# Two attentions on one core: V in products of 512 columns, PSUM banks shared, V moved to the start of a unit

## The chip, the core and the metric

The kernel runs on one core of a Trainium2 chip. The core has a matrix engine (TensorE, "PE" in the profile, with its weight loader "PEld" and its sequencer "PEq"), VectorE (DVE), ScalarE (ACT), GpSimd (POOL) and a queue engine (SyncE, SP). Transfers are issued from ScalarE's queue (ACTq) and SyncE's queue (SPq). Products go into PSUM, which has eight banks of 512 fp32 columns per partition; ScalarE and VectorE read them from there. The metric is the device time of one execution in microseconds (us), as the median over runs.

## The reference: two attentions, side by side

Two independent inputs x (2048 x 1024) each go through a projection to q, k and v, an attention with 32 heads of 32 columns, and an output projection; the two results are concatenated. They differ in which keys a query sees:

```python
# A: 8 keys, at distances 0, 2, 4 ... 14 behind the query
off = jnp.arange(W) * dil                      # W, dil = 8, 2
logits = jnp.einsum("bhsd,bhswd->bhsw", q, kg) * scale
logits = jnp.where(mask[None, None, :, :], logits, -1e9)
o = jnp.einsum("bhsw,bhswd->bhsd", _softmax(logits), vg)

# B: the 256 keys up to and including the query
mask = (idx[:, None] - idx[None, :] >= 0) & (idx[:, None] - idx[None, :] < W)   # W = 256
scores = jnp.where(mask[None, None], scores, -1e9)
o = jnp.einsum("bhqk,bhkd->bhqd", _softmax(scores), v)
# both: o.transpose(...).reshape(B, S, D) @ wo
```

## The kernel before

**Units and groups.** The work is cut into 8 units of 512 rows: four of B ("dense"), then four of A, whose rows are sorted into even and odd so that its 8 keys become neighbours ("window"). A unit has 8 groups (NG) of 4 heads. `attention` (L560) makes the steps of a group; `window` replaces its second half for A.

**Split products.** Each fp32 operand is split into a rounded high part and a low remainder (`parts`, L117: a cast on L120, a subtraction on L125 on GpSimd or L128 on VectorE). Each product is done three times (TERMS: high-high, high-low, low-high). Projections split weights and x; for the scores the three terms are stacked on 96 partitions by transfers on SyncE's queue (L308), so that one product does all of them.

**The steps.** `qk_items` (L343) computes q and k of a group: for each of them 8 slices of the contraction (NK), each of 3 products of 512 columns, into one bank. `evac` (L294, L298) takes them out and issues the stacking; parts of k that the next chunk needs go through `halo` buffers in DRAM (L288, L313). `v_items` (L387) computes V for two groups at a time, a "part": 8 slices, two banks, in each bank two row blocks of 256 columns, 3 products each. Here x is the stationary operand and the weights move. There are four parts to a unit; `vbuf` keeps six row blocks of each, since a dense chunk looks 256 rows back. `o_items` (L426) is the output projection of the unit before, 8 blocks of 8 slices.

**The attention of a group.** `first` (L585) makes 16 score tiles; each lies in a bank until VectorE has masked it and taken the row maximum (L590) and ScalarE has taken exp and its sum (L595). `log_sum` and `rows` (L608 to L631) bring the logarithms of the sums into two extra rows of the stacked q. `second` (L667, window L480) makes the scores again, transposed and already normalised; ScalarE takes exp (L672, L485), masks follow on VectorE or GpSimd (L653, L656, L495), and `values` (L712, L519) multiplies with V. `finish` (L548, L552) writes the split output `ot`.

**The order.** Nothing is scheduled at run time: while the kernel is built, a `Clock` keeps estimated times of all engines, and a loop at the end takes, out of four sequences (aux, second scores and values, first scores, projections), the item that is ready first; on a tie the projections come last. So projections fill the gaps between scores. The order of the projections is the list `plan`, made from `V_SLOTS = {0: 0, 1: 1, 5: 2, 7: 3}` (V part 0 after q and k of group 0, and so on) and `O_SLOTS`. `Stream` loads weights and x in that order through three raw buffers on ScalarE's queue (L94) and splits them a little ahead. `x_items` brings the next unit's x in the middle of the last V part.

**PSUM.** Seven banks are two rings: `rg`, three banks for projections, and `rs`, four banks for scores (`NS = 4`); the eighth, `ro`, takes the values.

Of the kernel before, what the change touches and what calls it, by code (L numbers as in the profile page):

```python
# [14 lines left out]
P = 128  # L15
# [64 lines left out]
class Stream:  # L80
# [10 lines left out]
    def load_to(self, n):  # L91
        while self.loaded < min(n, len(self.items)):
            raw = self.raws.tile([P, 1024], F32, tag="raw", name="raw")
            self.nc.scalar.dma_start(raw, self.items[self.loaded][1])  # L94
            self.raw[self.loaded] = raw, self.ck.load(1.9, self.ck.now)
            self.loaded += 1
# [20 lines left out]
    def parts(self, t, raw, t0):  # L117
        nc, ck = self.nc, self.ck
        n = raw.shape[1]
        nc.vector.tensor_copy(t[:, 0, :], raw)  # L120
        end = r = ck.use("dve", n / 1920 + 0.16, t0)
# [16 lines left out]
def kernel(ctx, tc, xs, wqk, wv, wo, outs, units):  # L138
# [14 lines left out]
    psg = ctx.enter_context(tc.tile_pool(name="psg", bufs=7 - NS, space=PSUM))  # L153
    pss = ctx.enter_context(tc.tile_pool(name="pss", bufs=NS, space=PSUM))
# [23 lines left out]
    def unit_x(u):  # L178
        for g in range(4):
# [6 lines left out]
    for p in plan:  # L186
# [3 lines left out]
        elif p[0] == "v":  # L190
            for g in range(2):
                item(p + (g,), "w", wv[ly, 2 * p[2] + g])
# [4 lines left out]
        else:  # L197
            item(("qk", p[1], 0, 0), "w", wqk[units[p[1]][0], 0])
            unit_x(p[1])
# [39 lines left out]
    vbuf = [const.tile([P, 6, 256], F32, name=f"vbuf{i}") for i in range(4)]  # L239
# [6 lines left out]


# [18 lines left out]
    rg, rs, ro = Ring(psg, 7 - NS, "g"), Ring(pss, NS, "s"), Ring(pso, 1, "o")  # L266
# [11 lines left out]
    def qk_items(u, s):  # L278
# [45 lines left out]
        for t in range(2):  # L324
# [13 lines left out]
            def run(k, t=t, h=h):  # L338
# [3 lines left out]
                for i, (a, b) in enumerate(TERMS):  # L342
                    nc.tensor.matmul(h["ps"], h["w"][:, a, k * P:(k + 1) * P], xt[u][k][:, b, :],  # L343
                                     start=(k == 0 and i == 0), stop=(k == NK - 1 and i == 2))
                if k == 3 and st.items[min(where["qk", u, s, t] + 1, len(st.items) - 1)][0] != "x":
# [21 lines left out]
    def v_items(u, part):  # L367
# [3 lines left out]
        h = {}  # L371

        def ready(k, b):
            if k % 4 == 0 and b == 0:
                st.split_to(where["v", u, part, k // 4] + 1)
                h["r"] = st.ready[where["v", u, part, k // 4]]
            return latest(h["r"], rg.when()) if k == 0 else h["r"]

        def run(k, b):
            if k == 0:  # L380
                h[b] = rg.take()
            if k % 4 == 0 and b == 0:
                h["w"] = st.get(where["v", u, part, k // 4])[0].rearrange("p a (k f) -> p a k f", k=4)
# [457 lines left out]
```

## Time and profile before

| | |
|---|---|
| median of 3 runs | 1996.71 us |
| the three runs | 1998.98, 1987.27, 1996.71 us |
| profiled execution, its own time | 1983.01 us |
| its span | 1980.9 us |
| mean granted TensorE clock | 0.987 |
| VectorE, ScalarE, GpSimd busy | 65%, 48%, 30% of the span |
| TensorE products | 12608 records |

Durations in the profile are of one execution. "Busy" is the time covered by an engine's instructions; a matrix product's bar is longer than the distance to the next one's start, since products are pipelined. A group's row gives the line and engine, output and input by the program's names, shapes, count, busy time, mean of one in ns, and the idle time before it with what ended it. In the timeline the columns are start, duration, engine, line, operation and count, with idle time before it in brackets. A window gives busy time and count of each engine, then the granted clock, the share of the transfer engines and GB/s.

### The profile page before, as it was taken

How to read it: one execution, taken by the hardware profiler on the slowest of the kernel's cores; microseconds unless marked ns; L12 is line 12 of the kernel's file. 1: busy time of each engine (PE TensorE's matmuls, PEld its weight loads, DVE VectorE, ACT ScalarE, POOL GpSimd, SP SyncE). 2: the span in 40 equal slices, each digit the busy share in tenths (PEclk: the TensorE clock that was granted, in tenths of full speed). 3: DMA queues.
4: the chain of work that ended last, by engine and by line, in shares of the span. 5: the costliest groups of instructions: out<-in, count | busy, mean ns of one | idle time of the engine just before them, and what ended most of it. 6: DMA issues, size and time to landing. Idle time of an engine off the chain costs nothing.

```text
span 1980.9 us, 36437 instructions
## 1 busy us (share of the span) xinstructions
PE 1925.2 (97%) x12608; PEld 1620.0 (82%) x12608; DVE 1284.9 (65%) x3700; ACT 952.4 (48%) x3125; POOL 593.0 (30%) x717
## 2 busy tenths in 40 slices
PE   8999999999999999999999999999999999999998
PEld 6877887888877888788888888978898888878886
DVE  5667775678775777566865667645686557655562
ACT  3466464566554656555563344423444334423441
POOL 3333333334333343433342221222222221222121
PEclk9999999999999999999999999999999999999998
DMA  5545546455446465344635546445563656444442
GB/s 175 155 125 141 178 123 177 133 162 168 120 142 186 123 184 137 119 147 146 170 114 150 165 151 188 130 132 172 145 190 114 181 165 180 138 146 134 141 137 75
DMA packets 136503, 294.93 MB, mean 149 GB/s; under 512 B 14464, under 2 KB 42112, under 8 KB 136320
## 3 DMA queue, kind: packets, MB, share of 16 engines
q1 hardware_dynamic: 85632, 124.82, 25.5%
q10 hardware_dynamic: 50688, 167.79, 24.5%
q8 instruction: 100, 1.64, 0.3%
q14 instruction: 83, 0.68, 0.1%
HBM read 163.58 MB, written 27.26 MB: 96 GB/s over the span
## 4 chain that ended last, share of the span: by engine, by line
PE 81%; DVE 9%; DMA 6%; ACT 2%; issue 2%; SPq 0%; ACTq 0%; DVEq 0%
PE g L343 31%; PE g L426 16%; PE g L387 14%; PE s L585 7%; PE s L667 4%; PE o L712 3%; PE s L480 3%; PE o L519 2%; DMA qst<-rt 2%; DVE x L128 1%; DVE w L120 1%; DVE w L128 1%; DMA kst<-nat 1%; ACT s L595 1%; DVE s L590 1%
## 5 line engine op out<-in xcount | busy, mean ns | idle before, releaser
L343 PE MATMUL g<-x,w 128*128 128x512 f32 x3072 | 797.7, 400 | 8.5 <-DVE w L120 8.1
L125 POOL TENSOR_TENSOR w<-raw,w 128x512 fp32r<-128x512 f32 x231 | 404.1, 1749 | 1127.1 <-DVE w L120 778.9
L343 PEld LDWEIGHTS g<-x,w 128*128 128x128 f32 x3072 | 561.2, 191 | 112.6 <-DVE w L120 8.4
L595 ACT ACTIVATE s<-s,nm 128x384 f32<-128x384 f32 (+3 forms) x1024 | 451.8, 442 | 287.0 <-DVE nm L590 271.6
L387 PE MATMUL g<-w,x 128*128 128x256 f32 x3072 | 412.7, 285 | 0.0
L426 PE MATMUL g<-ot,w 128*128 128x512 f32 x1536 | 391.5, 399 | 3.6 <-DVE w L120 2.9
L387 PEld LDWEIGHTS g<-w,x 128*128 128x128 f32 x3072 | 391.6, 191 | 2.0 <-issue 1.0
L426 PEld LDWEIGHTS g<-ot,w 128*128 128x128 f32 x1536 | 285.6, 191 | 57.5 <-DVE w L120 3.6
L590 DVE CUSTOM_DVE_ANT_0 s<-s,mask_d 128x384 f32<-128x384 f32 (+2 forms) x512 | 261.4, 556 | 77.2 <-PE s L585 76.1
L585 PE MATMUL s<-kst,qst 96*128 96x384 f32 (+3 forms) x1024 | 236.3, 304 | 22.4 <-issue 7.9
L653 POOL TENSOR_SCALAR_AFFINE_SELECT pbuf<-pbuf 128x128 f32<-128x128 f32 (+1 forms) x451 | 179.4, 419 | 193.7 <-ACT pbuf L672 188.7
L672 ACT ACTIVATE pbuf<-s 128x384 f32<-128x384 f32 (+2 forms) x480 | 198.8, 504 | 78.0 <-PE s L667 66.3
L585 PEld LDWEIGHTS s<-kst,qst 96*128 96x128 f32 x1024 | 180.3, 193 | 64.5 <-issue 21.7
L590 DVE CUSTOM_DVE_ANT_0 s<-s,mask_w 128x136 f32<-128x136 f32 (+1 forms) x512 | 142.4, 323 | 117.1 <-PE s L585 115.8
L595 ACT ACTIVATION_READ_ACCUMULATOR s<-s,nm 128x1 f32 x1024 | 209.8, 205 | 0.0
L120 DVE CAST w<-raw 128x1024 fp32r<-128x1024 f32 x256 | 197.5, 771 | 10.4 <-PE g L426 10.4
L128 DVE TENSOR_TENSOR w<-raw,w 128x512 fp32r<-128x512 f32 x281 | 195.0, 701 | 8.8
L294 ACT ACTIVATE nat<-g 128x512 fp32r<-128x512 f32 x128 | 76.6, 598 | 248.7 <-PE g L343 212.2
L298 DVE SCALAR_TENSOR_TENSOR nat<-g,nat 128x512 fp32r<-128x512 f32 x128 | 88.3, 690 | 152.2 <-ACT nat L294 136.8
L495 DVE TENSOR_TENSOR pbuf<-pbuf,keep_w 128x272 f32<-128x272 f32 (+1 forms) x224 | 116.2, 564 | 52.5 <-ACT pbuf L485 51.7
L590 DVE DVE_READ_ACCUMULATOR2_ANT nm<- 128x1 f32 x1024 | 145.1, 142 | 0.0
L667 PEld LDWEIGHTS s<-qst,kst 98*128 98x128 f32 x704 | 107.5, 189 | 40.7 <-ACT s L595 15.8
(44 smaller groups left out, 1050.7 us busy)
## 6 DMA issues: line engine op xcount, KB each, us to landing
raw<-wqk ACTq DMA_DIRECT2D x128, 512.0 KB
qst<-nat SPq DMA_DIRECT2D x192, 256.0 KB
kst<-nat SPq DMA_DIRECT2D x192, 256.0 KB
raw<-wv ACTq DMA_DIRECT2D x64, 512.0 KB
raw<-wo ACTq DMA_DIRECT2D x64, 512.0 KB
raw<-xs ACTq DMA_DIRECT2D x32, 512.0 KB
outs<-ost ACTq DMA_DIRECT2D x64, 256.0 KB
halo<-nat SPq DMA_DIRECT2D x40, 256.0 KB
```

The lines of the kernel that those rows point to most:

```text
L120: nc.vector.tensor_copy(t[:, 0, :], raw)
L125: nc.gpsimd.tensor_tensor(o, a, b, op=ALU.subtract)
L128: nc.vector.tensor_tensor(o, a, b, op=ALU.subtract)
L343: nc.tensor.matmul(h["ps"], h["w"][:, a, k * P:(k + 1) * P], xt[u][k][:, b, :], start=(k == 0 and i == 0), stop=(k == NK - 1 and i == 2))
L387: nc.tensor.matmul(h[b][0][:, 256 * r:256 * r + 256], xt[u][k][:, a, p0:p0 + P], h["w"][:, c, k % 4, :], start=(k == 0 and i == 0 and r == 0),
L426: nc.tensor.matmul(h["ps"], h["w"][:, a, k * P:(k + 1) * P], ot[u, k][:, b, :], start=(k == 0 and i == 0), stop=(k == NK - 1 and i == 2))
L585: nc.tensor.matmul(ps[:, :n], q[0:96, j, b * P:(b + 1) * P], kk[0:96, j, c0:c1], start=True, stop=True)
L590: nc.vector.tensor_tensor_reduce(ps[:, :n], ps[:, :n], mask[:, cut:full], scale=-1.0, scalar=BIG, op0=ALU.add, op1=ALU.min, accum_out=nm)
L595: nc.scalar.activation(ps[:, :n], ps[:, :n], AF.Exp, bias=nm, scale=-1.0, accum_out=sm)
L653: nc.gpsimd.affine_select(w, w, pattern=[[0, m], [step, n]], compare_op=ALU.is_ge, fill=0.0, base=base, channel_multiplier=chan)
L667: nc.tensor.matmul(ps[:, i * n:(i + 1) * n], kk[0:98, j, 256 + kb * P:256 + (kb + 1) * P], q[0:98, j, q0:q0 + n], start=True, stop=True)
L672: nc.scalar.activation(w, ps[:, :pack * n].rearrange("p (j n) -> p j n", j=pack), AF.Exp)
```

## The change

There are five edits, and their helpers.

1. **V in two parts of four groups.** `VPARTS = ((0, 4), (4, 4))`: a part has 8 slices and four banks, one row block of 512 columns in each, 3 products. The products go from 3072 of 256 columns to 1536 of 512. The weights are loaded as two half rows of two tiles.
2. **Seven banks shared.** `Banks` replaces the two rings: projections may hold all seven, scores up to `SMANY = 5`, or `SFEW = 3` while `narrow` is set (from the end of the q and k before a V part until that part's last bank is taken).
3. **V moved.** Part 0 opens each unit but the first, before q and k of group 0; part 1 follows group 5 (in the first unit, group 3). The last step of a V part also waits until the groups of the unit before that read those buffers are done.
4. **The last q and k side by side**, slice by slice, with the next unit's x between the slices, one load of x for every four items.
5. **Casts on ScalarE.** `parts` gives a cast to ScalarE where its estimate ends at least `ACT_BIAS` us earlier there. In the order that results, 18 of 320 casts move.

```diff
-NRAW, NP, NO, NS = 3, 768, 10, 4
+NRAW, NP, NO = 3, 768, 10
+SFEW, SMANY = 3,5
+ACT_BIAS = 1.0
+VPARTS = ((0, 4), (4, 4))
-V_SLOTS = {0: 0, 1: 1, 5: 2, 7: 3}
+V_SLOTS = {0: 0, 5: 1}
+V0_SLOTS = {3:1}
...
-        nc.vector.tensor_copy(t[:, 0, :], raw)
-        end = r = ck.use("dve", n / 1920 + 0.16, t0)
+        da, dv = n / 1200 + 0.1, n / 1920 + 0.16
+        if max(ck.free["act"], ck.now, t0) + da + ACT_BIAS <= max(ck.free["dve"], ck.now, t0) + dv:
+            nc.scalar.copy(t[:, 0, :], raw)
+            end = r = ck.use("act", da, t0)
+        else:
+            nc.vector.tensor_copy(t[:, 0, :], raw)
+            end = r = ck.use("dve", dv, t0)
...
+            ahead = u and s == 0
+            if s in V_SLOTS and ahead:
+                plan.append(("v", u, V_SLOTS[s]))
             plan.append(("qk", u, s))
-            if s in V_SLOTS:
+            if u == 0 and s in V0_SLOTS and s:
+                plan.append(("v", u, V0_SLOTS[s]))
+            elif s in V_SLOTS and not ahead and (u or not s):
                 plan.append(("v", u, V_SLOTS[s]))
...
+                    w4 = wv[ly, s0 + g // 2:s0 + g // 2 + 3:2, :, g % 2 * 512:g % 2 * 512 + 512]
+                    item(p + (g,), "w", w4.rearrange("t p c -> p t c"))
...
+    class Banks:
+        free, user = [0.0] * 7, [None] * 7
+        def __init__(self, tag, most):
+            self.tag, self.most = tag, most
+        def when(self):
+            known = sorted(t for t in self.free if t is not None)
+            if not known:
+                return None
+            t = known[0]
+            held = [f for f, w in zip(self.free, self.user) if w == self.tag and (f is None or f > ck.now)]
+            over = len(held) - self.most(ck) + 1
+            if over > 0:
+                ends = sorted(f for f in held if f is not None)
+                if len(ends) < over:
+                    return None
+                t = max(t, ends[over - 1])
+            return t
...
-    rg, rs, ro = Ring(psg, 7 - NS, "g"), Ring(pss, NS, "s"), Ring(pso, 1, "o")
+    narrow = [0]
+    rg, rs, ro = Banks("g", lambda ck: 7), Banks("s", lambda ck: SFEW if narrow[0] else SMANY), Ring(pso, 1, "o")
...
+            if k == NK - 1 and u and any((u - 1) * NG + i not in done["o"] for i in range(s0, s0 + ng)):
+                return None
...
+                narrow[0] = ng == 4 and b < nb - 1
...
-            for r in range(2):
+            for r in range(per):
                 for i, (a, c) in enumerate(TERMS):
-                    p0 = (2 * b + r) * P
-                    nc.tensor.matmul(h[b][0][:, 256 * r:256 * r + 256], xt[u][k][:, a, p0:p0 + P],
-                                     h["w"][:, c, k % 4, :], start=(k == 0 and i == 0 and r == 0),
+                    p0 = (per * b + r) * P
+                    ps = h[b][0] if per == 1 else h[b][0][:, 256 * r:256 * r + 256]
+                    nc.tensor.matmul(ps, xt[u][k][:, a, p0:p0 + P],
+                                     h["w"][:, c, k % kw], start=(k == 0 and i == 0 and r == 0),
...
+            if NG - 1 not in V_SLOTS and p[2] == NG - 1 and p[1] + 1 < U:
+                new = [new[t * NK + k] for k in range(NK) for t in range(2)]
+                for g, x in reversed(list(enumerate(x_items(p[1] + 1)))):
+                    new[4 * g:4 * g] = x
```

More of the change, by code (lines that the diff above doesn't have):

```diff
@@ L245, with take, give @@
         done[k] = {}
+    class Banks:
[15 more added lines that the diff above has]
+            return t
+        def take(self):
+            i = min((t, i) for i, t in enumerate(self.free) if t is not None)[1]
+            self.free[i], self.user[i] = None, self.tag
+            return psb.tile([P, 512], F32, tag=f"b{i}", name=self.tag), i
+        def give(self, i, t):
+            self.free[i] = t
     class Ring:
@@ L401, in v_items @@
         for k in range(NK):
-            for b in range(2):
-                out.append((lambda k=k, b=b: ready(k, b), lambda k=k, b=b: run(k, b), 3 * CV,
+            for b in range(nb):
+                out.append((lambda k=k, b=b: ready(k, b), lambda k=k, b=b: run(k, b), 3 * (CV if ng == 2 else CG),
                             lambda k=k, b=b: after(k, b)))
@@ L464, in window @@
         q, kk = qst[buf], kst[buf]
-        v = vbuf[s // 2]
-        vc = (s % 2) * P
+        vp, vc = vpart[s]
+        v = vbuf[vp]
         two = []
@@ L699, in values_ready @@
                 return None
-            if (u, s // 2) not in done["v"] or any(h.get(("left", k, pr), 1) for k in ks for pr in range(2)):
+            if (u, vp) not in done["v"] or any(h.get(("left", k, pr), 1) for k in ks for pr in range(2)):
                 return None
-            return latest(done["v"][u, s // 2], ro.when() if ks[0] == 0 else 0.0,
+            return latest(done["v"][u, vp], ro.when() if ks[0] == 0 else 0.0,
                           *[h["pr", k, pr] for k in ks for pr in range(2)])
```

73 lines of the change are left out of this document (46 added, 27 removed).

## The prediction

> **What bounds the kernel now.** I read the page first (busy time and clock, then the chain that ended last), then the groups by line, then the timeline of TensorE and the windows.
>
> ```profile
> span 1980.9 us, 36437 instructions
> PE 1925.2 (97%) x12608; PEld 1620.0 (82%) x12608; DVE 1284.9 (65%) x3700; ACT 952.4 (48%) x3125; POOL 593.0 (30%) x717
> PE 81%; DVE 9%; DMA 6%; ACT 2%; issue 2%; SPq 0%; ACTq 0%; DVEq 0%
> L343 PE MATMUL g<-x,w 128*128 128x512 f32 x3072 | 797.7, 400 | 8.5 <-DVE w L120 8.1
> L387 PE MATMUL g<-w,x 128*128 128x256 f32 x3072 | 412.7, 285 | 0.0
> L426 PE MATMUL g<-ot,w 128*128 128x512 f32 x1536 | 391.5, 399 | 3.6 <-DVE w L120 2.9
> ```
>
> TensorE is busy for 97% of the span and carries 81% of the chain; no other engine passes 65%. So only three things pay: fewer TensorE nanoseconds per product, fewer waits in its fixed order, and fewer stretches at a reduced clock. The busy sums cannot give the price of one product, since a product's bar (400 or 285 ns) overlaps the next one's. I take the pitch, from start to start.
>
> ```profile
> core 0: us, PE busy (x) PEld busy (x), PEclk, DMA share, GB/s
> 24.00:29.00 5.00, 5.00 (x44) 5.00 (x43) 1.00 1.00 258
> 1312.00:1319.00 7.00, 7.00 (x33) 5.78 (x31) 1.00 1.03 281
> ...
> 395.41 0.86 PE L343 MATMUL g<-x,w 128*128 128x512 f32 x3
> 396.11 0.69 PE L585 MATMUL s<-kst,qst 96*128 96x384 f32 x3
> ...
> 399.15 0.87 PE L387 MATMUL g<-w,x 128*128 128x256 f32 x6
> 399.86 0.34 PE L585 MATMUL s<-kst,qst 96*128 96x384 f32 x1
> ```
>
> The first window holds V products alone, the second output products of 512 columns alone. With one bar's length added for the overlapping ends, V costs (5.00 + 0.285)/44 = 120 ns for 256 columns, the other (7.00 + 0.40)/33 = 224 ns for 512. In the first the weight loader is busy all 5.00 us, in the second 5.78 of 7.00: V at 256 columns leaves the loads no room. Between scores the difference is small: six V products take 399.86 - 399.15 = 0.71 us, three of 512 take 396.11 - 395.41 = 0.70 us.
>
> **The change part by part.** The sums are made against the profiled execution, 1983.0 us (1980.9 of span and 2.1 outside it). The three timed runs have a median of 1996.7 us, a factor 1.0069 above it.
>
> *V at 512 columns.* 3072 products become 1536, with the same columns and half the weight loads. Saved per pair: 2 x 120 - 224 = 16 ns in long stretches (1536 x 16 = 25 us), (0.71 - 0.70)/3 = 3 ns between scores (5 us). V runs mostly in pieces between scores, and the order of the changed kernel cuts it finer still, so I take the lower half: 12 us saved, bounds 5 and 25. The Trainium skill ("TensorE: Matmul & The Clock Gate", section "Back-to-back issue gap") gives N/2.4 + 2.5 ns, so that a pair of 256 would exceed one of 512 by an estimated 2.5 ns, 1536 of which are 4 us: by that rule the sum below would be 8 us poorer. The loader's full 5.00 us in the V window, which that formula leaves out, speaks for more.
>
> *Narrow scores between wide products.* The instruction order of the changed kernel has the 1600 score products of up to 256 columns in 547 unbroken runs instead of 445.
>
> ```profile
> 1870.20 1.00 PE L480 MATMUL s<-qst,kst 98*128 98x136 f32 x8
> 1871.05 0.92 PE L387 MATMUL g<-w,x 128*128 128x256 f32 x6
> ...
> 1898.97 0.23 PE L585 MATMUL s<-kst,qst 96*128 96x136 f32 x1
> 1899.03 0.91 PE L343 MATMUL g<-x,w 128*128 128x512 f32 x3
> ```
>
> Eight in a row take 0.85 us, 106 ns each; one alone behind a projection product takes 0.06 us. A new cut saves about 46 ns: 102 x 46 ns = 5 us, bounds 0 and 5.
>
> *Seven shared banks.* Scores had four banks; they now have up to five outside the long V parts and three inside, projections whatever is free.
>
> ```profile
> PEld s L667 <- ACT s L595: 15.8, 30, 1.2
> PEld s L585 <- ACT s L595: 9.7, 31, 1.7
> PE s L585 <- ACT s L595: 2.7, 3, 1.2
> ```
>
> The loader waits 25.5 us for a bank that ScalarE has yet to release, and of that only some 3 us are bare idle of TensorE. A fifth bank can save 3 to 25 us; I take 5, near TensorE's own row. The three banks are the second rival.
>
> *Stalls at the end of long stretches.* TensorE's order is fixed when the kernel is built. Where no scores are ready, a long stretch of projections is laid out, then the first scores at the moment their transfer should have landed; if it lands late, TensorE stands.
>
> ```profile
> 1322.75 1.09 PE L585 MATMUL s<-kst,qst 96*128 96x136 f32 x4 [3.38 <-issue]
> 1782.90 1.09 PE L585 MATMUL s<-kst,qst 96*128 96x136 f32 x4 [3.63 <-issue]
> ...
> 1320.00:1325.00 5.00, 2.25 (x7) 2.02 (x8) 1.14 (x8) 1.36 (x8) 0.00 (x0) 0.66 0.25 91
> 1325.00:1330.00 5.00, 5.00 (x19) 4.14 (x18) 1.61 (x10) 1.29 (x6) 0.00 (x0) 0.65 0.00 0
> ```
>
> In the windows the clock is the third number from the end. After 3.38 us of idle it is 0.66 and 0.65, which costs up to another 5 x 0.34 + 5 x 0.35 = 3.4 us. Two such stalls make some 14 us. At the pitches above, and passing over the single small product of the row sums, stretches of projections worth over 15 us number 12 in the order before and 4 in the order after. If two stalls in three go with them, 9 us are saved. Nothing proves that shorter stretches stall less: bounds 20 saved and 10 lost.
>
> *The start.* The changed kernel casts the second x tile on ScalarE and subtracts it on GpSimd; VectorE no longer does both before the first weight cast.
>
> ```profile
> 6.32 0.42 DVE L120 CAST x<-raw 128x512 fp32r<-128x512 f32 x1
> 6.78 0.69 DVE L128 TENSOR_TENSOR x<-raw,x 128x512 fp32r<-128x512 f32 x1
> 7.39 0.69 DVE L120 CAST w<-raw 128x1024 fp32r<-128x1024 f32 x1
> 8.13 6.96 PE L343 MATMUL g<-x,w 128*128 128x512 f32 x16 [8.13 <-DVE w L120]
> ```
>
> The cast at 7.39 can begin at 6.32, so TensorE starts 1 us sooner. The other 17 moved casts lie on ScalarE at 48% busy, at nothing.
>
> *The end loses its filler.* Before, the last unit closes with a V part between the last Q and K and the output products; now V stands earlier and the output products follow at once.
>
> ```profile
> 1902.37 1.65 PE L387 MATMUL g<-w,x 128*128 128x256 f32 x12
> 1909.93 0.56 PE L585 MATMUL s<-kst,qst 96*128 96x136 f32 x4
> 1924.39 0.22 PE L585 MATMUL s<-kst,qst 96*128 96x136 f32 x1
> 1936.84 3.23 PE L426 MATMUL g<-ot,w 128*128 128x512 f32 x6 [0.70 <-ACT ot L548]
> ...
> L590 DVE CUSTOM_DVE_ANT_0 s<-s,mask_w 128x136 f32<-128x136 f32 (+1 forms) x512 | 142.4, 323 | 117.1 <-PE s L585 115.8
> L590 DVE DVE_READ_ACCUMULATOR2_ANT nm<- 128x1 f32 x1024 | 145.1, 142 | 0.0
> L495 DVE TENSOR_TENSOR pbuf<-pbuf,keep_w 128x272 f32<-128x272 f32 (+1 forms) x224 | 116.2, 564 | 52.5 <-ACT pbuf L485 51.7
> ```
>
> From the last K to the closing output products it takes 1936.84 - 1902.37 = 34.5 us, of which 96 x 120 ns = 11.5 us are V: 23 us without it. After the change, the last group's scores come 1909.93 - 1902.37 = 7.6 us after the last K, as before; the order puts all 16 of them and the previous group's second scores side by side with no filler, so VectorE paces them: 16 x (323 + 142) + 7 x 564 ns = 11.4 us; from the last of them to the closing products 1936.84 - 1924.39 = 12.4 us as before. That makes 31.4 us against 23: 8 us lost, bounds 3 (VectorE not the pace) and 12 (a further stall at a low clock).
>
> *At nothing.* The x loads move from the last V part to the last Q and K, side by side: 48 products of 224 ns are 10.8 us of cover, V had 11.5; and the new unit opens with V, which uses a pair of x tiles in 24 products (5.4 us) where Q used them in 6. If that cover failed, the opening V part would wait for a transfer at each of seven boundaries. The V weights now come in rows half as long, on the same ScalarE queue; a tile feeds 24 products, 5.4 us, and three raw buffers run ahead. A new guard holds V's last step until the four groups whose values it overwrites are done; these belong to the unit before, and TensorE's other work does not queue behind it, since the order has them first. The 64 copies out of PSUM keep their size.
>
> **Sum:** -12 - 5 - 5 - 9 - 1 + 8 = -24 us: 1983.0 - 24 = 1959 us on the profiled scale, times 1.0069 gives 1973 us beside the median.
>
> **The rivals.** *A: only arithmetic.* Late transfers, not long stretches, make the stalls, and they move elsewhere; banks give nothing. For it: the waits at 1322 and 1782 are for issue, not for an engine. Then -12 - 5 - 1 + 8 = -10 us: 1987 us.
>
> *B: three banks hold the scores back.* In the V parts a score tile may take one of three banks only.
>
> ```profile
> 43.80 0.34 PE L585 MATMUL s<-kst,qst 96*128 96x384 f32 x1
> 45.80 0.54 ACT L595 ACTIVATE s<-s,nm 128x384 f32<-128x384 f32 x1
> ...
> L590 DVE CUSTOM_DVE_ANT_0 s<-s,mask_d 128x384 f32<-128x384 f32 x448 | 240.1, 581 | 64.6 <-PE s L585 63.7
> ```
>
> A tile holds its bank from 43.80 to 46.34, 2.5 us, here behind a weight cast on VectorE; three banks pass one tile in 0.85 us, VectorE one in 581 + 142 = 723 ns. If all of the 0.13 us came onto TensorE's path, some 20 tiles in each of 16 V parts would cost 42 us: 1983 - 24 + 42 = 2001, or 2015 us. It decides from about 75 ns a tile, where the 24 us are gone. Against it: not every hold lies behind a cast, and 12 products of V fill the time between tiles.
>
> *C: clock.* Cycling through four banks breaks TensorE's stream so that the clock drops. If each V part lost what the window from 1325 lost, 1.75 us, 16 of them cost 28 us: 1987, or 2001 us. Against it: V already alternates two banks at 1.00 in the window at 24 us. The Trainium skill (the same page, section "A second HAM failure mode: psum-queue depth-cycling") reports such a case; no run here shows it yet.
>
> **How the numbers follow.** About 1% (20 us) is what a measurement of this kernel tells from no change: the three runs lie 12 us apart. The forecast has 0.63 (its own range 1950 to 1985, with 0.53 of it below 1977), A 0.22, B 0.12, C 0.03. Faster 0.53; same 0.10 + 0.22 = 0.32; slower 0.15. The range goes from 1948 (the stalls and banks at their better bounds in part) to 2005, which takes in A and C and the milder half of B.
>
> **What would show it.** V's pitch near 225 to 235 ns, and the loader no longer full there; some 12 us less of projection work in all; no idle of over 3 us in the window units; from the last K to the closing output products 31 us; the first product at 7 us. I am wrong if scores in V parts wait for ScalarE by more than 75 ns a tile, if new stalls stand where units meet, or if the clock falls in V.

## The result and the profile after

The changed kernel took 2103.23 us (median of four runs, 2096.83 to 2109.39) against 1997.72 us before: a ratio of 1.054, 95% interval 1.0492 to 1.0588. It is slower, and lies 98 us above the top of the forecast's range. The profiled execution took 2104.23 us, with a span of 2102.5 us and a mean granted clock of 0.960.

From the page of the changed kernel: busy times, the chain that ended last, and the groups of TensorE (line and shapes, then busy time, mean ns, idle time before and what ended most of it).

```profile
span 2102.5 us, 33627 instructions
PE 1962.0 (93%) x11072; PEld 1569.6 (75%) x11072; DVE 1274.4 (61%) x3684; ACT 993.4 (47%) x3156; POOL 610.8 (29%) x702
...
PE 68%; DMA 17%; DVE 9%; ACT 2%; issue 2%; SPq 1%; POOL 0%; ACTq 0%; DVEq 0%; POOLq 0%
...
L455 PE MATMUL g<-w,x 128*128 128x512 f32 x1536 | 424.4, 409 | 1.4 <-POOL w L135 0.5
...
L654 PE MATMUL s<-kst,qst 96*128 96x384 f32 (+3 forms) x1024 | 258.0, 312 | 89.9 <-DMA kst<-nat 28.4
```

VectorE, the next engine, is busy for 61%. What changed is the chain: 17% of it are transfers, where it was 6%, and the first scores (L654, before L585) have 89.9 us of idle time ahead of them. The waits of TensorE say what for; the columns are us in total, times, and the longest. First the changed kernel, then the kernel before.

```profile
PE s L654 <- DMA kst<-nat: 28.4, 11, 5.9
PE s L654 <- DMA halo<-nat: 22.7, 8, 6.5
PE s L654 <- issue: 20.6, 8, 6.7
PE s L736 <- DMA qst<-rt: 12.5, 9, 3.7
PE s L549 <- DMA qst<-rt: 11.7, 6, 5.1
PE s L654 <- DMA qst<-nat: 9.4, 2, 5.2
```

```profile
PE s L585 <- issue: 7.9, 3, 3.6
...
PE s L585 <- DMA kst<-nat: 5.3, 5, 1.5
PE s L667 <- DMA qst<-rt: 4.0, 5, 1.3
PE s L480 <- DMA qst<-rt: 3.9, 4, 1.4
...
PE s L585 <- DMA halo<-nat: 2.0, 2, 1.3
```

All six lines are waits of scores for the stacking of q and k or for the row sums: 105.3 us, against 23.1 us in the same places before. (An `issue` line names no releaser.) Without the wait for the first weights, TensorE stands for more than 2 us at 24 places; before it was 4. By the semaphores' updates in the trace, 20 of the 24, `issue` and `halo` ones too, end within 0.4 us after a k transfer (15) or the row sums (5) landed. One lies within 10 us before each of the seven unit starts (2.0 to 5.7 us; 1035.62, 1285.22 and 1538.02 are three of them), others just after a start (1559.94, 1795.52) and where output products are laid out (367.01, 614.20, 924.72).

One of them, in TensorE's timeline and in windows of 1 us (the clock is the third number from the end, then the share of the transfer engines):

```profile
604.08 3.61 PE L398 MATMUL g<-x,w 128*128 128x512 f32 x15
614.20 0.66 PE L654 MATMUL s<-kst,qst 96*128 96x384 f32 x1 [6.50 <-DMA halo<-nat]
```

```profile
609.00:610.00 1.00, 0.00 (x0) 0.00 (x0) 0.00 (x0) 0.00 (x0) 0.00 (x0) 1.00 1.08 375
610.00:611.00 1.00, 0.00 (x0) 0.00 (x0) 0.00 (x0) 0.00 (x0) 0.00 (x0) 0.60 0.99 397
...
614.00:615.00 1.00, 0.80 (x3) 0.69 (x4) 0.10 (x1) 0.00 (x0) 0.00 (x0) 0.50 0.02 7
...
619.00:620.00 1.00, 1.00 (x5) 0.90 (x4) 0.09 (x1) 0.41 (x1) 0.00 (x0) 0.50 0.08 16
620.00:621.00 1.00, 1.00 (x5) 0.81 (x5) 1.00 (x5) 1.00 (x4) 0.00 (x0) 0.78 0.00 0
621.00:622.00 1.00, 1.00 (x9) 0.89 (x7) 1.00 (x3) 0.91 (x5) 0.00 (x0) 1.00 0.00 0
```

TensorE stands 6.5 us, then works at half clock from 614.2 until past 620: 3.1 us more are lost. The queue that brings the operands, SyncE's, in the same stretch, then its third k transfer and the load of ScalarE ahead of it:

```profile
594.88 1.87 SPq L363 DMA_DIRECT2D qst<-nat  x3
596.80 4.74 SPq L343 DMA_DIRECT2D kst<-halo  x3
602.90 6.03 SPq L363 DMA_DIRECT2D kst<-nat  x3
608.99 0.59 SPq L368 DMA_DIRECT2D halo<-nat  x1
```

```profile
608.39 0.55 SPq L363 DMA_DIRECT2D kst<-nat  x1
603.10 0.36 ACTq L99 DMA_DIRECT2D raw<-wo  x1
```

The ten transfers of the group start at 594.88, and the scores can start at 614.20, 19.3 us later. The profile puts this wait down to the halo store, but the semaphores that the score waits for tell of the k transfers. The last of these three was issued at 608.39, when the weight load that ScalarE had issued at 603.10 had landed (608.37), and itself landed at 614.11. The two share a semaphore: the program has eight of them for the landings of both queues' transfers, and an issue waits until the transfer that had its semaphore before has landed.

The order was made with a reckoning of these times. Its lines: SyncE issues a transfer in 0.63 us after the eighth transfer before it, of either queue, has landed (`lands[-8]`); 0.4 us later it moves for the time given with it (0.95 us for a stacking, more while loads move too), and its data count as landed `LAND = 0.45` us after that. That is 2.4 us from issue to landing for a transfer that meets no other. By the semaphores' updates in the traces, the median of the 192 k transfers is 4.4 us before and 5.5 us after. The coupling of the two queues shows in SyncE's waits, of the changed kernel, then of the kernel before:

```profile
SPq L363 <- DMA raw<-wo: 40.8, 10, 6.0
SPq L363 <- DMA raw<-wv: 36.2, 9, 8.4
SPq L363 <- DMA raw<-xs: 35.3, 11, 5.4
SPq L363 <- DMA raw<-wqk: 33.5, 12, 4.3
...
SPq L363 <- DMA outs<-ost: 23.4, 8, 6.9
```

```profile
SPq L308 <- DMA raw<-wv: 46.5, 14, 8.0
...
SPq L308 <- DMA raw<-xs: 11.2, 2, 6.7
...
SPq L308 <- DMA outs<-ost: 4.7, 5, 1.8
```

SyncE stands behind loads and stores of ScalarE's queue; over all its lines but the closing one that is 255 us after, 164 before. Counted in SyncE's timeline, the issue of one group's k transfers, with the halo store behind them, takes over 10 us in 17 of 64 groups, before in 8.

**An account.** Three parts make up the span: the time in which TensorE stood (span less PE's busy time on the page), the clock lost while it worked (in windows of 1 us, busy time times one less the granted clock), and the remainder, called work here.

| us | span | stood | clock lost | work |
|---|---|---|---|---|
| before | 1980.9 | 55.7 | 23.0 | 1902.2 |
| after | 2102.5 | 140.5 | 69.8 | 1892.2 |

The work fell by 10.0 us, the way the change meant; standing rose by 84.8 and the lost clock by 46.8. The remainder is no exact price of the products, though: it also differs by some 10 us between orders of the same products (1902.2, 1904.7 and 1915.3 us for the kernel before, e5 and e18 in the table below).

### The profile page after: what moved, and what is told of

It reads as the page before. It is cut to its first block, busy times and chain, and to the rows that moved or that the text cites. A ratio compares the mean times of both kernels' runs of the same rounds, so it can differ in the third digit from the quotient of the medians.

```text
span 2102.5 us, 33627 instructions
## 1 busy us (share of the span) xinstructions
PE 1962.0 (93%) x11072; PEld 1569.6 (75%) x11072; DVE 1274.4 (61%) x3684; ACT 993.4 (47%) x3156; POOL 610.8 (29%) x702
## 4 chain that ended last, share of the span: by engine, by line
PE 68%; DMA 17%; DVE 9%; ACT 2%; issue 2%; SPq 1%; POOL 0%; ACTq 0%; DVEq 0%; POOLq 0%
PE g L398 23%; PE g L495 14%; PE g L455 13%; PE s L654 6%; PE s L736 4%; DMA kst<-nat 4%; PE o L781 3%; DMA qst<-rt 3%; DMA halo<-nat 3%; PE s L549 3%; DMA raw<-wo 2%; PE o L588 2%; DMA qst<-nat 1%; DVE w L130 1%; DMA raw<-wv 1%
## 5 line engine op out<-in xcount | busy, mean ns | idle before, releaser
L398 PE MATMUL g<-x,w 128*128 128x512 f32 x3072 | 815.1, 406 | 8.1 <-DVE w L130 7.5
L135 POOL TENSOR_TENSOR w<-raw,w 128x512 fp32r<-128x512 f32 x240 | 420.4, 1752 | 1109.8 <-DVE w L130 767.3
L398 PEld LDWEIGHTS g<-x,w 128*128 128x128 f32 x3072 | 572.5, 195 | 117.4 <-DVE w L130 7.8
L664 ACT ACTIVATE s<-s,nm 128x384 f32<-128x384 f32 (+3 forms) x1024 | 451.9, 442 | 405.3 <-DVE nm L659 381.7
L455 PE MATMUL g<-w,x 128*128 128x512 f32 x1536 | 424.4, 409 | 1.4 <-POOL w L135 0.5
L495 PE MATMUL g<-ot,w 128*128 128x512 f32 x1536 | 404.0, 403 | 5.2 <-DVE w L130 3.6
L654 PE MATMUL s<-kst,qst 96*128 96x384 f32 (+3 forms) x1024 | 258.0, 312 | 89.9 <-DMA kst<-nat 28.4
L455 PEld LDWEIGHTS g<-w,x 128*128 128x128 f32 x1536 | 283.1, 195 | 51.1 <-POOL w L135 2.0
L654 PEld LDWEIGHTS s<-kst,qst 96*128 96x128 f32 x1024 | 193.2, 200 | 152.4 <-issue 87.1
L722 POOL TENSOR_SCALAR_AFFINE_SELECT pbuf<-pbuf 128x128 f32<-128x128 f32 (+1 forms) x410 | 156.9, 398 | 238.9 <-ACT pbuf L741 229.9
L664 ACT ACTIVATION_READ_ACCUMULATOR s<-s,nm 128x1 f32 x1024 | 206.9, 202 | 0.0
L736 PE MATMUL s<-qst,kst 98*128 98x256 f32 (+2 forms) x704 | 141.0, 307 | 13.4 <-DMA qst<-rt 12.5
```

The source lines that it names most:

```text
L135: nc.gpsimd.tensor_tensor(o, a, b, op=ALU.subtract)
L455: nc.tensor.matmul(ps, xt[u][k][:, a, p0:p0 + P], h["w"][:, c, k % kw], start=(k == 0 and i == 0 and r == 0), stop=(k == NK - 1 and i == 2 ...
L495: nc.tensor.matmul(h["ps"], h["w"][:, a, k * P:(k + 1) * P], ot[u, k][:, b, :], start=(k == 0 and i == 0), stop=(k == NK - 1 and i == 2))
L654: nc.tensor.matmul(ps[:, :n], q[0:96, j, b * P:(b + 1) * P], kk[0:96, j, c0:c1], start=True, stop=True)
L664: nc.scalar.activation(ps[:, :n], ps[:, :n], AF.Exp, bias=nm, scale=-1.0, accum_out=sm)
L722: nc.gpsimd.affine_select(w, w, pattern=[[0, m], [step, n]], compare_op=ALU.is_ge, fill=0.0, base=base, channel_multiplier=chan)
```

## The experiments

Each was run beside the kernel before on the same chip; the ratio is to that. The kernel before had medians of 1987 to 1992 us in these runs and of 1997.72 beside the changed kernel, so differences between the changed kernel's 2103.23 us and the medians below are up to 10 us larger than what the ratios give. The table has the three parts of the account for each. (Some expectations speak of "idle", the idle times in brackets summed over the timeline, which is close to "stood", and of a "rest" in which clock lost during idle time was also taken off; its differences were therefore too large, 24 us where "work" gives 9.)

| run | median | ratio, interval | stood | clock lost | work |
|---|---|---|---|---|---|
| e1_dve_casts | 2120.53 | 1.0651, 1.056–1.0741 | 147.2 | 75.6 | 1893.0 |
| e2_whole_rows | 2088.73 | 1.0491, 1.0409–1.0573 | 138.0 | 55.6 | 1893.9 |
| e3_old_v | 2040.46 | 1.0249, 1.0168–1.0329 | 100.7 | 31.0 | 1907.1 |
| e4_late_after | 2027.09 | 1.0181, 1.0093–1.027 | 95.1 | 41.6 | 1885.4 |
| e5_late_before | 1971.95 | 0.9916, 0.9884–0.9947 | 48.4 | 17.2 | 1904.7 |
| e6_old_v_caps | 2007.73 | 1.0096, 1.0058–1.0133 | 78.2 | 31.6 | 1897.7 |
| e7_rows_late | 2016.31 | 1.0139, 1.0071–1.0206 | 91.1 | 41.3 | 1887.1 |
| e8_rows_later | 2001.46 | 1.0082, 1.002–1.0145 | 76.9 | 33.0 | 1889.8 |
| e9_four_banks | 2085.74 | 1.0495, 1.0465–1.0526 | 136.3 | 59.6 | 1887.7 |
| e11_outs_pool | 2065.43 | 1.0393, 1.031–1.0476 | 117.7 | 44.4 | 1894.7 |
| e12_caps_dve | 1983.51 | 0.9957, 0.993–0.9984 | 62.8 | 18.2 | 1898.6 |
| e13_place_256 | 2051.51 | 1.0323, 1.0293–1.0353 | 96.9 | 47.4 | 1905.3 |
| e14_same_order_256 | 2053.24 | 1.0322, 1.0221–1.0423 | 103.8 | 51.8 | 1901.1 |
| e15_no_reserve | 2081.59 | 1.0465, 1.038–1.055 | 119.9 | 66.8 | 1895.3 |
| e16_serial_last | 2088.73 | 1.0501, 1.035–1.0652 | 142.0 | 64.2 | 1891.1 |
| e17_all_late | 2001.14 | 1.0053, 1.0029–1.0077 | 78.5 | 35.7 | 1888.3 |
| e18_later_before | 1980.48 | 0.995, 0.9917–0.9983 | 45.2 | 18.2 | 1915.3 |
| e19_later_256 | 2007.69 | 1.0073, 1.005–1.0096 | 71.7 | 35.0 | 1899.3 |

### One part undone

**Casts back on VectorE**: `ACT_BIAS` so high that none moves.

```diff
-ACT_BIAS = 1.0
+ACT_BIAS = 1.0e9
```

> The changed kernel with every cast back on VectorE. In the changed kernel ScalarE waits 36 us in 11 waits for x before a cast that stands in its order, with the evictions of q and k and the raw loads behind it. If that blockade makes the late stacking transfers (theory 'ScalarE's queue'), the time falls by 30 us or more from 2103, to 2070 or less, and TensorE's idle from 143 us to 110 or less. If the stalls come from an order laid out too tightly (theory 'tight order') or from the V loads (theory 'half rows'), the time stays at 2090 to 2115.

It is not faster but, if anything, slower (1.0651 against 1.054, intervals that overlap a little). The moved casts are not what costs in this design.

**V weights in whole rows**: the host lays the same weights out so that a V tile is one contiguous load.

```diff
-item(p + (g,), "w", w4.rearrange("t p c -> p t c"))
+item(p + (g,), "w", wv[ly, s0 + g])
...
```

> The changed kernel with the V weights laid out beforehand, so that each load is one whole row of 4 KB per partition as before the change, and the same bytes. Theory 'half rows': the 8192 additional packets delay the stacking transfers; then the time falls by 30 us or more, to 2070 or less. Theories 'tight order' and 'ScalarE's queue': the share of the transfer engines falls by about 2 points, the time stays within 2085 to 2110.

TensorE's order is the same as in the changed kernel. 14.5 us less in the median, but the intervals overlap; the standing time hardly moves. At most a minor cost.

**The old V**: four parts of 256 columns at their old places, the last q and k as before; shared banks and casts stay.

```diff
-VPARTS = ((0, 4), (4, 4))
+VPARTS = ((0, 2), (2, 2), (4, 2), (6, 2))
-V_SLOTS = {0: 0, 5: 1}
-V0_SLOTS = {3:1}
+V_SLOTS = {0: 0, 1: 1, 5: 2, 7: 3}
+V0_SLOTS = {1: 1, 5: 2, 7: 3}
...
-            ahead = u and s == 0
+            ahead = False
...
```

> The changed kernel with V as before the change: four parts of 256 columns in the old places, the x loads in the last V part, q and k of the last group one after the other; the shared banks and the casts on ScalarE stay. If the new place and size of V make the stalls, the time returns to 1980 to 2005 and TensorE's idle to 40 to 60 us. If the shared banks (finer order of scores) or the casts make them, it stays above 2060 with idle over 100 us.

This wins back 63 us (58 by the ratios) and leaves 2.5% against the kernel before, although here the products are as before: its work is 4.9 us above, and the other 53 us of its span's excess are standing and lost clock. So V's move and width carry the larger half of the loss, and the banks and casts the rest.

### The allowance for landing

**Later landing, in the changed kernel and in the kernel before**: the only edit is what the reckoning adds to each transfer.

```diff
-TAIL, LAND, XAT = 2, 0.45, 1
+TAIL, LAND, XAT = 2, 2.5, 1
```

> The changed kernel with one number of the planner changed: it takes every transfer to land 2.5 us after its bytes instead of 0.45, so that first scores are laid out about 2 us later behind other work. Theory 'tight order' (transfers land later than estimated, TensorE's fixed order has no slack): TensorE's idle falls from 143 us to 90 or less and the time by 40 us or more, to 2060 or less. If the transfers are late because the order itself holds them back (a queue, a buffer not yet free), the scores only move further and the time stays at 2085 to 2120.

> The kernel before with the same number of the planner changed as in the run that brought the changed kernel to 2027 us (landing 2.5 us instead of 0.45). Theory 'tight order, made by the new plan': the old order has slack where the transfers land, so the number gives little: 1970 to 2000 us, within 1% of before. Rival 'the planner is too hopeful everywhere': it gains here as it did there in proportion to the idle (50 us against 143), some 20 us or more, to 1970 or less.

The changed kernel loses 76 us of its time (71 by the ratios) through this one number: standing 140.5 to 95.1, clock lost 69.8 to 41.6. The products are the same in another order; with it some small steps changed their engine (GpSimd has 471 masks instead of 426). So a large part of the stalls comes of scores that stand in the order before their operands arrive. That it is not the luck of one order the other runs below bear out: five orders of the new design with 0.45 us took 2082 to 2121 us (the changed kernel, e1, e9, e15, e16), three with more 2001 to 2027. The kernel before gains too, 0.8%, and is then faster than both kernels of this study. Its waits for transfers:

```profile
PE s L585 <- DMA qst<-rt: 4.4, 1, 4.4
PE s L585 <- DMA kst<-nat: 3.9, 2, 3.0
...
PE s L585 <- issue: 3.1, 5, 1.9
...
PE s L480 <- DMA qst<-rt: 1.8, 2, 1.1
```

13.2 us (and 0.3 at L667) where there were 23.1 with an allowance of 0.45, although 13 of its 64 groups take over 10 us to issue k and the halo store, and SyncE stands 235 us behind loads and stores of ScalarE, nearly as long as in the changed kernel. Slow issues alone don't make TensorE stand; an order that allows for them stands less for transfers.

**With whole rows, 2.5 us and 4.5 us; and the kernel before with 4.5 us**, the same edits together (`LAND` 2.5 in e7, 4.5 in e8 and e18).

> The changed kernel with both remedies: whole rows for the V weights (alone -15 us) and landing 2.5 us in the planner (alone -76 us). If they act on the same late transfers they don't add up: 2010 to 2027 us. If each has its own part, 2005 to 2015 us.

> As the run before, with landing 4.5 us. Theory 'tight order': the transfers are late by up to 6 us, so more allowance still gains, to 2000 us or less, TensorE's idle below 80 us and the clock above 0.98. If 2.5 us was already enough, the planner now leaves gaps or holds loads back: 2020 us or more.

> The kernel before with a landing allowance of 4.5 us in place of 0.45; no other edit. Theory (transfers that land later than the order assumes make the stalls in both kernels, and 2.5 us removed most of them from the kernel before, at 1972 us): little is left to win, 1965 to 1980 us, idle 30 to 42 us. Rival (late transfers still cost at 2.5 us): below 1962 us, idle under 30 us. Second rival (a longer allowance puts the scores too late and costs cover elsewhere): above 1985 us.

The changed kernel comes down to 2001 us. Its waits then:

```profile
PE s L692 <- DVE hl L684: 16.6, 9, 3.8
PE s L653 <- DMA kst<-nat: 16.5, 7, 3.9
...
PE s L653 <- DMA raw<-wv: 7.2, 2, 4.4
```

A new wait leads, for the row sums on VectorE (L692, 16.6 us). For the kernel before, 4.5 us is no better than 2.5 (0.995 and 0.9916, intervals that overlap): it stands 3 us less, but its work is 11 us more. So the best order found of the old design is some 1.4% ahead of the best one found of the new (e17).

### Banks, places, queues

**Four banks, or no reserve, for scores**: the limits of `Banks` alone.

```diff
-SFEW, SMANY = 3,5
+SFEW, SMANY = 3, 4
```

```diff
-SFEW, SMANY = 3,5
+SFEW, SMANY = 5, 5
```

> The changed kernel with scores capped at four banks instead of five (three inside V parts, as it was). With V as before, five banks in place of four and projections capped at three made 2008 into 2040 us. If the fifth bank does the same here, the time falls by some 30 us, to 2060 to 2085, with fewer waits of TensorE on transfers. If the place of V makes the stalls by itself, the time stays within 15 us of 2103.

> The changed kernel without the limit of three banks for scores around V parts; a V part takes its four banks as they come free, so that it starts a little later. If holding the scores back there makes the stalls (my second rival), the time falls by 20 us or more, to 2080 or less. If it does not, 2085 to 2120 us.

Neither moves the result clearly (1.0495 and 1.0465 beside 1.054, intervals that overlap). Three banks in the V parts are not the main cause: by the ratios, 15 us would hang on them here, which is within the intervals.

**Old V with four score banks and three for projections, casts on ScalarE or not**: e3 with the shares of the kernel before, but any free bank instead of a ring; e12 also without the moved casts.

```diff
-SFEW, SMANY = 3,5
+SFEW, SMANY = 4, 4
-rg, rs, ro = Banks("g", lambda ck: 7), Banks("s", lambda ck: SFEW if narrow[0] else SMANY), Ring(pso, 1, "o")
+rg, rs, ro = Banks("g", lambda ck: 3), Banks("s", lambda ck: SFEW if narrow[0] else SMANY), Ring(pso, 1, "o")
```

> V as before the change, and the shared banks capped so that scores take at most four and projections at most three, as before; only the casts on ScalarE and the free choice of a bank stay. V as before with five banks for scores took 2040 us, 50 above before. If the fifth bank makes that, the time is 1980 to 2005 and TensorE's idle 60 us or less. If the casts on ScalarE or the choice of banks make it, it stays at 2025 to 2050.

> V as before, caps of four and three banks as before (2008 us with casts on ScalarE), and all casts on VectorE: what is left of the change is that a free bank is chosen by time, not in a ring. If the casts on ScalarE made the 20 us over before, the time is 1980 to 1998. If the free choice (another order of the same work) makes them, it stays at 2000 to 2020.

e12 is in essence the kernel before with a free choice of bank: 0.9957, a small gain. With the casts it is 24 us slower (e6). With five banks for scores and up to seven for projections it is another 33 us slower (e3, 1.0249 beside 1.0096, intervals apart). In the changed kernel the casts were no loss (e1), and four banks for scores no clear gain (e9). So an edit's worth hangs on the order around it.

**V at its new places, but 256 columns**: two parts of two groups, one after the other, where a part of four stood; the limit of three banks never sets in, and the weights come in whole rows.

```diff
-VPARTS = ((0, 4), (4, 4))
-V_SLOTS = {0: 0, 5: 1}
+VPARTS = ((0, 2), (2, 2), (4, 2), (6, 2))
+V_SLOTS = {0: (0, 1), 5: (2, 3)}
...
```

> The changed kernel with V in products of 256 columns, two parts one after the other at each of the new places, scores at five banks throughout. The 512 columns should save 10 to 25 us of arithmetic, and their three banks for scores may cost some. If the place makes the stalls, the time is 2100 to 2130, with idle of 120 us or more. If the wide parts (four banks held, three left) make them, it falls below 2070.

Within 11 us of e3 (1.0323 and 1.0249, intervals that just overlap) and 52 us under the changed kernel: the new places are not the main part of V's loss. The width is the main suspect, which the pair further down tests alone.

**Output stores on GpSimd's queue**, TensorE's order unchanged.

```diff
-nc.scalar.dma_start(outs[u, n], o)
+nc.gpsimd.dma_start(outs[u, n], o)
```

> The changed kernel with the 64 stores of the output issued from GpSimd's queue instead of ScalarE's. In the changed kernel SyncE's queue, which carries the stacking, waits 305 us for raw loads and output stores before it may issue (164 us before the change), 76 us of them for stores (5 before). Theory 'shared slots': these waits make the stacking late; without the stores they fall by some 70 us, TensorE's idle by 20 us or more and the time to 2075 or less. If SyncE's waits are hidden (the stacking waits for a free buffer anyway), the time stays at 2090 to 2115.

38 us less, 29 by the ratios (1.0393, upper end 1.0476, against a lower end of 1.0492): standing 140.5 to 117.7, clock lost 69.8 to 44.4. The stores now have semaphores of their own, and SyncE's waits for loads and stores of ScalarE fall from 255 to 186 us. With the order fixed, sharing landings with the other queue is what the edit takes from the stores; it costs, and the prediction had left it out. (The 305 and 76 us of the expectation hold the closing wait of 50 us, which its 164 and 5 leave out.)

**The last q and k one after the other again**, x between the slices of k.

```diff
-new = [new[t * NK + k] for k in range(NK) for t in range(2)]
 for g, x in reversed(list(enumerate(x_items(p[1] + 1)))):
-    new[4 * g:4 * g] = x
+    new[NK + 2 * g:NK + 2 * g] = x
```

> The changed kernel with q and then k of a unit's last group one after the other, as before, and the x loads among the slices of k only. TensorE stands 2 to 6 us shortly before six of seven unit starts in the changed kernel. If the side by side with its x loads makes that, the stalls there go and the time falls by 20 to 40 us, to 2060 to 2085. If opening a unit with V behind any x load makes them, the time stays at 2090 to 2120.

Inconclusive: 1.0501, interval 1.035 to 1.0652; standing as in the changed kernel.

**All three remedies**: whole rows, 4.5 us, stores on GpSimd's queue.

> The changed kernel with all three remedies that helped alone: whole rows for V, landing 4.5 us in the planner (together 2001 us), and the output stores on GpSimd's queue (alone -38). If the stores still hold the stacking up, 1975 to 1992 us, level with or below before; if the allowance already covers that, 1995 to 2010 us.

No clear gain over the same without the stores (1.0053 beside 1.0082): in this order, with slack, they cost nothing that shows.

### Width alone, in one and the same order

**Each V product as two of 256 columns into the halves of its bank**; all else, and the order, as in the changed kernel (e14), and as in e8 with its allowance of 4.5 us (e19).

```diff
...
-                    nc.tensor.matmul(ps, xt[u][k][:, a, p0:p0 + P],
-                                     h["w"][:, c, k % kw], start=(k == 0 and i == 0 and r == 0),
+                    for e in range(2):
+                        nc.tensor.matmul(h[b][0][:, 256 * e:256 * e + 256], xt[u][k][:, a, p0:p0 + P],
+                                         h["w"][:, c, k % kw, e], start=(k == 0 and i == 0 and e == 0),
...
```

> The changed kernel, its order untouched, but each V product of 512 columns issued as two of 256 into the halves of the same bank. Only the arithmetic saving goes. If span less idle less lost clock (1875 us in the changed kernel, 1903 before) is the arithmetic, it rises by 15 to 28 us. If the stalls come from the order, the idle stays at 120 to 145 us and the time rises to 2110 to 2130. If TensorE had simply become too fast for the transfers, the saving is given back as idle: the time stays within 5 us of 2103 and the idle falls by as much as the arithmetic rises.

> Whole V rows and a landing allowance of 4.5 us (the version that took 2001 us), but each V product issued as two of 256 columns into the halves of the same bank, the order of everything else unchanged. Theory (with the tight order, wide products lose because an order built without slack turns their saving into stalls on transfers): with the allowance, the stalls are mostly gone at both widths, so the wide products should now keep most of their saving of some 24 us, and this run should be slower than 2001 us: 2010 to 2025 us, its idle within 15 us of the 72 us there. Rival (wide products drive TensorE past its transfers whatever the allowance): this run is faster than 2001 us, 1975 to 1998 us, with idle below 55 us.

This is the pair that tells most. The narrow form makes 8.9 us more work, as it should, and yet is 2% faster in the order of the changed kernel: standing 140.5 to 103.8, clock lost 69.8 to 51.8, together 54.7 us. The waits of e14 are at the same places of the order as in the changed kernel, fewer or shorter on the whole: 15 over 2 us instead of 24.

```profile
PE s L654 <- DMA kst<-nat: 31.8, 12, 5.7
PE s L654 <- issue: 12.8, 8, 5.4
PE s L549 <- DMA qst<-rt: 8.0, 2, 4.2
...
PE s L736 <- DMA qst<-rt: 7.7, 5, 3.6
...
PE s L654 <- DMA halo<-nat: 4.6, 2, 3.3
```

64.9 us for these five, where the changed kernel has 95.9. With the allowance of 4.5 us the pair no longer differs: work 9.5 us less at 512 columns, standing and clock together 3.2 us more, and ratios of 1.0082 and 1.0073. So neither expectation for e19 was met in its time; that the standing would be the same at both widths was. Wide products lose in the order without slack; in the other they keep in the profile 6.3 us of span, which the timed runs cannot tell from nothing.

## Why the prediction was wrong

**The step that failed is "Stalls at the end of long stretches".** It took the two idles it showed as a matter of long stretches of projections, counted fewer of these in the new order, and put down 9 us saved, bounds 20 saved to 10 lost. It measured 84.8 us more standing and 46.8 us more clock lost. The stretches did become fewer, 12 to 4 as counted, but the idles of over 2 us rose from 4 to 24. What makes a stall is not the length of the stretch ahead of it, but that the order places a score where the reckoning has its operands landed, 0.45 us after the move, while the queues bring them later. In the kernel before this left 23 us of waits for transfers; each new order has its own, and 2.5 us of allowance take 71 us by the ratios off the changed kernel.

**Rival A had the mechanism and not the price.** It says that late transfers make the stalls and that they move elsewhere, but reckons that they would stay as many as they were. A change that takes time out between transfers and the scores that wait for them can be paid back in stalls, and e14 against the changed kernel shows it: 9 us of work saved, 55 us given back.

**"At nothing" failed for the queues.** The prediction looked at what x and V weights would do to the products that use them, which was right (V's products wait 1.4 us in all), and not at the transfers of SyncE's queue, which stand behind ScalarE's loads and stores: 255 us of such waits for 164. The stores alone, taken to another queue, gave 29 us by the ratios (e11). The sum of such waits is no price by itself, since e5, the fastest run, has 235 us of them. Two of the prediction's own signs of being wrong came: a stall ahead of each of the seven places where units meet, and eight idles of over 3 us before scores in the window units, where it expected none. The moved casts cost nothing in the changed kernel (e1), but 24 us in another order (e12 to e6); the five banks cost 33 us with the old V (e6 to e3), where 5 saved were forecast.

**V at 512 columns was right.** A window of V products in the changed kernel:

```profile
504.50:508.50 4.00, 4.00 (x19) 3.25 (x19) 1.54 (x6) 0.89 (x3) 1.64 (x1) 1.00 1.07 258
```

(4.00 + 0.409)/19 = 232 ns, in the forecast's 225 to 235; the loader is busy 3.25 of 4.00 us, no longer all of it. The saving is 8.9 us of work in one pair of runs and 9.5 in the other, for the 12 forecast, bounds 5 and 25. By the formula that the Trainium skill ("TensorE: Matmul & The Clock Gate", section "Back-to-back issue gap") gives for an isolated product, it would have been an estimated 4 us; the traces show twice that.

**Narrow scores and the fifth bank gave nothing that shows.** Work fell by 10.0 us, of which the width explains 9; 5 us for longer runs of score products can't be told apart in a remainder that differs by as much between orders. TensorE waits 3.7 us for a score bank of ScalarE (L664), before 2.7, and the loader 22.9 for 25.5: 5 us were forecast.

**The start and the end came near, in part by luck.** The first product starts at 7.46 us for 8.13 (forecast 7): the first weight cast begins at 5.93 for 7.39, sooner than forecast, but takes 1.48 us for 0.69. The end:

```profile
2025.85 0.91 PE L398 MATMUL g<-x,w 128*128 128x512 f32 x3
...
2058.95 0.49 PE L495 MATMUL g<-ot,w 128*128 128x512 f32 x1 [0.70 <-ACT ot L617]
```

From the last K (2025.85 + 0.91) to the closing output products are 32.2 us; the forecast had 31.4. The parts differ: 6.9 us to the first score of the last group, 8.6 to the last, 16.7 from there, for 7.6, 11.4 and 12.4. The scores were not at VectorE's pace, and TensorE ran at half clock from 2037 until past 2050, so the sum came out by errors that cancel.

**Rivals B and C did not happen at their price.** B's was a wait of scores for ScalarE in the V parts; it is the 3.7 us above, at most 12 ns for each of some 320 tiles, and more banks for scores change nothing clearly (e15). C's clock is 1.00 in the window of V. At two unit starts (1293.59, 1785.03) V does begin at half clock, just after 1.1 us of waits of scores for ScalarE; that is 4.8 us of the lost clock. Some 59 of its 69.8 us lie in half clock that sets in during a single idle of over 1 us or right after it.

**What stays open.** Why the give-back is six times the saving: that the half clock after each stall delays the next group's operands or scores, so that one stall makes the next, would fit, and wasn't isolated. One more difference is on record: in the same order the transfers land sooner beside the narrow products, 4.6 us from issue to landing in the median of the k transfers in e14, 5.5 in the changed kernel. Why, the runs don't show. How much of the 29 us between e5 and e8 belongs to the new places and how much to the order that the builder happened to find wasn't told apart either.

## What to carry to other kernels

Where an order is fixed when the kernel is built, a saving on the busiest engine counts only if the order allows for when transfers really land: read the waits for transfers and their number before costing the arithmetic, and count each transfer queue as part of the path. Before judging such a change, give the order more allowance in both versions; here one constant was worth over 70 us in the changed kernel and turned the kernel before into the fastest of the study. To price one edit, hold the order fixed and change only that, as the same products in two widths did.

## What the runs showed of the hardware

**Short idles halve the clock.** The prediction had seen it after 3.4 us. Here 1.81 us suffice; the timeline and windows of 2 us around it:

```profile
1180.48 0.66 PE L654 MATMUL s<-kst,qst 96*128 96x128 f32 x2 [1.81 <-DMA kst<-nat]
```

```profile
1179.00:1181.00 2.00, 0.52 (x3) 0.55 (x3) 0.03 (x1) 0.00 (x0) 0.00 (x0) 0.81 0.95 357
1181.00:1183.00 2.00, 2.00 (x7) 1.61 (x7) 1.45 (x7) 0.43 (x1) 0.00 (x0) 0.50 0.13 43
1183.00:1185.00 2.00, 2.00 (x6) 1.61 (x5) 0.03 (x1) 1.21 (x7) 0.00 (x0) 0.50 0.35 131
1185.00:1187.00 2.00, 2.00 (x8) 1.61 (x7) 1.52 (x6) 0.81 (x4) 0.26 (x1) 0.50 0.00 0
1187.00:1189.00 2.00, 2.00 (x12) 1.70 (x11) 0.92 (x6) 0.46 (x2) 1.49 (x1) 0.99 0.02 4
```

Over six microseconds at half clock follow, 3.2 us of TensorE time for a wait of 1.81. It isn't certain each time: an idle of 2.91 us that ended at 888.34 left the clock at 1.00. Of the idles of 1.4 us and more, most cost another 1.5 to 3.2 us in this way. The 27 stretches at half clock that end within this trace each last 3.41 us or two, three or four times that. Three of them set in without an idle of over 1 us, behind several short ones that sum to 0.8 to 1.3 us in the 3.41 us before.

**A transfer queue can wait for another engine's transfers.** SyncE's issues stood 255 us for loads and stores that ScalarE had issued, and moving the stores to a third queue cut TensorE's standing, which has nothing to do with them, from 140.5 to 117.7 us (e11). It is the program that ties the queues, by the eight semaphores they share; a limit of the chip is not shown.
